# Pairing the 64-token tails of two batches in the channel mix, under a new instruction order

## The chip, the cores and the metric

The kernel runs on one NeuronCore of a Trainium2 chip. The metric is the device time of one execution in microseconds (us). Four runs of the kernel before gave a median of 247.99 us (247.12 to 249.25). The profile is of one further execution.

The engines named below are TensorE (PE in the profile, its weight loads PEld), VectorE (DVE), ScalarE (ACT), GpSimd (POOL) and SyncE (SP). SP does no arithmetic here: it issues every transfer, DMA transposes included, one after the other from one queue.

## The reference

Eight batches of 576 tokens go through an attention of eight heads (a pooled part and a band of seven neighbours) that gives `x`, of 576 tokens by 512 channels. The second half mixes tokens and then channels:

```
theta = x @ w_theta
zr, zi = x * cos(theta), x * sin(theta)
y = einsum('ts,bsd->btd', w_tok_r, zr) + einsum('ts,bsd->btd', w_tok_i, zi)
u = x + y
out = u + maximum(u @ w_ch, 0.0)
```

The change concerns the last line, for tokens 512 to 575 of each batch.

## The kernel before

The work of a batch is cut into small steps. Each kind of step is a generator that walks over all batches in turn, and has one letter. The string `ORDER` says which generator makes its next step; `pin()` then ties every new instruction behind the one before it on the same engine. So `ORDER` fixes the order of the instructions on each engine and of the transfers on SP's queue, and a waiting instruction holds up all that stand behind it on its engine. A step is written here as letter, batch and number: R2.4 is the fifth step of R for batch 2.

| letter | step | engines |
|---|---|---|
| L, v | load of two heads of q or k (8 a batch), of a chunk of v (5) | SP |
| C, w | casts of these to bf16 | POOL (q of batch 0: ACT) |
| A | transposes of q and k, and their pooled sums (4) | PE in batches 0 to 5, ACT, DVE |
| Q, B, N | pooled scores (2), pooled values (1), pooled output (3) | PE, ACT, DVE, POOL |
| S | band scores of a chunk of keys, exponential, two selects that cut the band out (5) | PE, ACT, POOL (not batch 0) |
| V, T | band output of a chunk (5), its transpose and sum into `x` (5) | PE, DVE (POOL for T of 6 and 7) |
| H, Z, z | theta with its sine and cosine (5), products with x (4), turn of the tail's product (1) | PE, ACT, DVE, SP |
| X | token mix: four steps of nine 128x512 matmuls, and one of 36 matmuls for the 64-token tail | PE, DVE |
| u | DMA transposes of u, for the residual (2) | SP |
| R | channel mix of a chunk of tokens (5) | PE |
| O | maximum, residual, store of a chunk (5) | DVE, SP |
| l, c, W, h, g, D, K | weights (loads, casts, turns), warm-up matmuls, constants | all |
| q, t, x | DMA transposes in place of PE ones, batches 6 and 7 | SP |

A batch's 576 tokens are four chunks of 128 and a tail of 64. `mix` (X, L615) adds x to the token mix and leaves `u`, transposed, in `uT`: 512 tokens of four channel blocks, and behind them the four tails. `u_turn` (u, L634) turns both parts back with two DMA transposes (L639, L641). `channels` (R, L646) takes a chunk as the stationary operand: a full chunk needs four 128x512 matmuls (L653). The tail has only 64 columns, so two halves of the output's channels are put at partitions 0 to 63 and 64 to 127 of the same PSUM tile, in eight matmuls of 256 columns (L661). `store` (O, L668) has one DVE instruction a chunk (L675), 512 wide, or 256 wide for the tail, and one store (L681), or two for the tail (L684), each of 64 tokens by two runs of 128 channels.

PSUM and result tiles are few. `w1` hands out four one-bank tiles in rotation (H, T, X, R, Z, W, B and the last step of N), `w2` two two-bank tiles (A, S, Q, V and the first steps of N): a step can't begin on PE before the step that had its tile has been read out. The result tile `osb` of O has four buffers, free again when the store has landed. ScalarE holds one function table: it loads another (`ACT_TABLE_LOAD`) where S or Q follows H, and where H follows S or Q.

Of the kernel before, what the change touches and what calls it, by code (L numbers as in the profile page):

```python
# [10 lines left out]
BF16 = mybir.dt.bfloat16  # L11
AF = mybir.ActivationFunctionType
ALU = mybir.AluOpType
AX = mybir.AxisListType

P = 128
B = 8
H = 8
S = 576
# [22 lines left out]
HALF = 64  # L42
MAIN = 512
# [4 lines left out]
def kernel(  # L48
# [11 lines left out]
    nc = tc.nc  # L60
# [5 lines left out]
    moep = ctx.enter_context(tc.tile_pool(name="moep", bufs=2))  # L66
# [9 lines left out]
    def w1(name, dt=FP32):  # L76
        return ps1.tile([P, 512 if dt == FP32 else 1024], dt, tag="w1" + next(turn1), name=name)


    ORDER = (  # L80
        "LKLLLLLKKCLCCAvCCLvCDwvvvKLCAACwwwwLASCLSVQQCBlLLLLLVSlllllNvlCCCCNlvvvACNVCcScwcvTlTTccllcwAASlHVVH"
        "wwwDTTcAHZHZcHSZcccSDDhLLLzBcCSCWQDVWWLghLLLLCWCCvQvWWLNCNCCWWSWvvLvZNVVXwwwvAAvhwhTXTAALXSwSLLLLXQQ"
        "TBCCVgLggHCuLLVTvHNTVHHZNCCHCCCSwzZZZARRvvvSwOROALSXOLLAAXLLwSwwLvCCCCSCCCCRSNVOXVVXQVTTTAABwSXuTLLA"
        "vvwuvQRvvLLSTSHONNHVLLXuZZANHCLwHwwLVVHRQRRCCCCOzvLLLBOOCCSSTZTCvvRwOTLZSQHVHNVTXTAAXLLACACwCHHwCLCq"
        "LwwqNVHXSZNVXZZvvzSLLCCQCLqXVZLqQvRvwBvOVTVuTTLXTAwASSCHCCHCHNNXqvLwwTwuVXLVLAAHHXqSSZXRQROzONZSCCQC"
        "TCZBSVqROqvvvvZTSSROTVHVRHOTNNTXAAHVHHVwwwwwXAtAXSSzXXSSZZNZVuRuuRRROOQQtOOBRVRVttROtTTTOZOSTNXVRTuN"
        "RRxSSOOOHHVVXtttVHZHZZHNVzZXXttXuXTTXXHTHTTRxROOZHHRuROOHZRZZzOXXXXXXXRuRRRuuOORRuOOROROOORROO"
    )

    staged = {}  # L90
# [86 lines left out]
    for i in range(2):  # L177
        t = const.tile([P, 4, 5, KP], BF16, name=f"kdP{i}")
# [4 lines left out]
    for i in range(2):  # L183
        t = const.tile([P, 4, 5 * 120], BF16, name=f"kT{i}")
# [4 lines left out]
    for i in range(2):  # L189
        t = const.tile([P, NCH, H, 66], BF16, name=f"v_w{i}")  # L190
# [4 lines left out]
    for c in range(NCH):  # L195
        t = const.tile([P, DM], BF16, name=f"tmp{c}")
# [4 lines left out]
    for i in range(2):  # L201
        t = const.tile([P, 2, H, 66], BF16, name=f"vd{i}")
# [12 lines left out]
    wch = wpool.tile([P, 4, DM], BF16, name="wch")  # L215
# [305 lines left out]
    def parted(t):  # L521

        return (t[:, 0:4 * MAIN].rearrange("p (e t) -> p e t", e=4),
                t[:, 4 * MAIN:4 * S].rearrange("p (e t) -> p e t", e=4))
# [85 lines left out]
            yield  # L610


    uTs, urs = {}, {}

    def mix(b):  # L615

        (xA, xB), z = parted(xTs[b]), zs.pop(b)
        uT = uTs[b] = moep.tile([P, 4 * S], BF16, tag="uT", name=f"uT{b}")
        uA, uB = parted(uT)
        for dc in range(4):  # L620
            ps = w1(f"psu{dc}_{b}")
            for j in range(9):
                nc.tensor.matmul(out=ps, lhsT=z[:, j, P * dc:P * dc + P], rhs=WT[:, j, 0:MAIN], start=(j == 0), stop=(j == 8))  # L623
            nc.vector.tensor_tensor(out=uA[:, dc, :], in0=ps, in1=xA[:, dc, :], op=ALU.add)  # L624
            yield
        ps = w1(f"psut_{b}")[:, 0:4 * HALF].rearrange("p (e t) -> p e t", e=4)
        for dc in range(4):
            for j in range(9):
                nc.tensor.matmul(out=ps[:, dc, :], lhsT=z[:, j, P * dc:P * dc + P], rhs=WT[:, j, MAIN:S],  # L629
                                 start=(j == 0), stop=(j == 8))  # L630
        nc.vector.tensor_tensor(out=uB, in0=ps, in1=xB, op=ALU.add)
        yield

    def u_turn(b):  # L634

        ur = moep.tile([P, 16, P], BF16, tag="ur", name=f"ur{b}")
        utr = moep.tile([P, 2, P], BF16, tag="utr", name=f"utr{b}")
        urs[b] = ur, utr
        nc.sync.dma_start_transpose(out=ur, in_=uTs[b][:, 0:4 * MAIN])  # L639
        yield  # L640
        nc.sync.dma_start_transpose(out=utr, in_=uTs[b][:, 4 * MAIN:4 * S])  # L641
        yield

    rels = {}

    def channels(b):  # L646

        uA, uB = parted(uTs[b])
        for c in range(5):
            psr = rels[b, c] = w1(f"psr{c}_{b}")  # L650
            if c < 4:
                for dc in range(4):
                    nc.tensor.matmul(  # L653
                        out=psr, lhsT=uA[:, dc, P * c:P * c + P], rhs=wch[:, dc, :],
                        start=(dc == 0), stop=(dc == 3),
                    )
            else:

                for dc in range(4):
                    for hf in range(2):  # L660
                        nc.tensor.matmul(  # L661
                            out=psr[64 * hf:64 * hf + 64, 0:256], lhsT=uB[:, dc, :],
                            rhs=wch[:, dc, :].rearrange("p (j e d) -> p e j d", j=2, e=2)[:, hf],
                            start=(dc == 0), stop=(dc == 3),
                        )
            yield

    def store(b):  # L668

        ur, utr = urs.pop(b)  # L670
        for c in range(5):
            psr = rels.pop((b, c))
            osb = moep.tile([P, DM], FP32, tag="osb", bufs=4, name=f"osb{c}_{b}")
            n = 4 if c < 4 else 2
            nc.vector.scalar_tensor_tensor(  # L675
                out=osb[:, 0:P * n].rearrange("p (e d) -> p e d", d=P),
                in0=psr[:, 0:P * n].rearrange("p (e d) -> p e d", d=P), scalar=0.0,
                in1=ur[:, c:16:4, :] if c < 4 else utr, op0=ALU.max, op1=ALU.add,
            )
            if c < 4:  # L680
                nc.sync.dma_start(out=out[b, P * c:P * c + P, :], in_=osb)  # L681
            else:
                for hf in range(2):
                    nc.sync.dma_start(  # L684
                        out=out[b, 512:576, :].rearrange("t (j e d) -> e t j d", j=2, e=2)[hf],
                        in_=osb[64 * hf:64 * hf + 64, 0:2 * P].rearrange("p (j d) -> p j d", j=2),
                    )
            yield

    last = {}
# [13 lines left out]
    def batches(steps):  # L709
        for b in range(B):  # L710
            yield from steps(b)

    sequences = dict(L=batches(load), v=batches(load_v), C=batches(cast), w=batches(cast_v), A=batches(turns), B=batches(pooled_v), Q=batches(scores), S=batches(band_scores), N=batches(pooled_out), q=batches(turn_qk), t=batches(turn_x), x=batches(turn_z),
                     V=batches(outputs), T=batches(transposes), H=batches(phases), Z=batches(modulate),
                     K=constants(), z=batches(z_turn), u=batches(u_turn), X=batches(mix), R=batches(channels), O=batches(store),
                     l=weight_loads(), c=weight_casts(), h=channel_loads(), g=channel_casts(), W=weight_turns(), D=warm_up())
    pin()
# [35 lines left out]
```

## Time and profile before

| | |
|---|---|
| median of four runs | 247.99 us |
| the profiled execution: its time | 247.94 us |
| its span, first to last instruction | 246.2 us |
| DVE, ACT, POOL busy | 186.0, 167.0, 161.8 us |
| matmuls of the whole token mix, L623, 288 of them | 66.3 us busy |
| matmuls of the channel mix, full chunks, L653, 128 of them | 31.3 us busy |
| `osb` by DVE, 512 wide, 32 of them | 686 ns each |
| `osb` by DVE, 256 wide, 8 of them | 418 ns each |
| issue of a tail store on SP, L684, 16 of them | 592 ns (median) |
| issue of a full store on SP, L681, 32 of them | 390 ns (median) |
| issue of a tail's transpose on SP, L641, 8 of them | 1193 ns (median) |

The span is 1.7 us shorter than the execution's time. "Busy" is time with at least one instruction of the engine running; a matmul's duration in the groups (379 ns) is longer than the distance from one start to the next (0.216 us for 128x512), because matmuls overlap in the array. The chain of waits gives the distance, and sums are made with it.

### The profile page before, as it was taken

The numbers are of one execution on the slowest core, as the hardware profiler recorded it, in microseconds if no ns is written. First come the engines' busy times: TensorE is split into PE (matmuls) and PEld (weight loads), VectorE is DVE, ScalarE is ACT, GpSimd is POOL, SyncE is SP. The second block draws the span as 40 slices with busy tenths as digits, with TensorE's granted clock in tenths as the row PEclk, the third lists the DMA queues.
The fourth block names the chain that finished last, engine by engine and source line by source line (L and its number), as shares of the span: only waits on it lengthen the run. The fifth ranks groups of instructions, "written<-read, shape, count | busy, mean of one in ns | idle before, by whom it ended". The sixth has DMA issues, their size and how long they took to land. (4 is left out here: it accounts for less than half of the span.)

```text
span 246.2 us, 6608 instructions
## 1 busy us (share of the span) xinstructions
PE 223.4 (91%) x2602; PEld 134.2 (54%) x2602; DVE 186.0 (76%) x345; ACT 167.0 (68%) x248; POOL 161.8 (66%) x223
## 2 busy tenths in 40 slices
PE   0777799999999999999999998999699999999990
PEld 0434554765566567656666555665455655455540
DVE  5275979679879898897989977997687776256462
ACT  3786799757998379998878999899924490350000
POOL 4466477998999999989858764996396943400000
PEclk9999999999999999999999999999989999999999
DMA  6999999999999999999999999199769594946496
GB/s 211 298 270 381 310 212 303 315 232 222 301 214 237 345 229 158 287 255 292 226 186 213 255 227 272 47 201 202 120 156 166 149 209 94 165 166 83 93 260 202
DMA packets 100511, 53.94 MB, mean 219 GB/s; under 512 B 83968, under 2 KB 86016, under 8 KB 100480
## 3 DMA queue, kind: packets, MB, share of 16 engines
q1 hardware_dynamic: 100480, 53.53, 93.8%
q8 instruction: 20, 0.33, 0.6%
q14 instruction: 11, 0.09, 0.2%
HBM read 33.59 MB, written 9.44 MB: 175 GB/s over the span
## 5 line engine op out<-in xcount | busy, mean ns | idle before, releaser
L623 PE MATMUL psu<-WT,z 128*128 128x512 bf16 x288 | 66.3, 379 | 0.5 <-ACT cs L568 0.5
L445 POOL TENSOR_SCALAR_AFFINE_SELECT pm<-pm 128x1024 bf16<-128x1024 bf16 (+1 forms) x35 | 36.8, 1051 | 18.5 <-ACT pm L438 18.5
L438 ACT ACTIVATE pm<-psS 128x1024 bf16<-128x1024 f32 (+1 forms) x40 | 37.7, 980 | 11.6 <-PE psS L430 10.7
L623 PEld LDWEIGHTS <-z 128*128 128x128 bf16 x288 | 26.8, 98 | 29.2 <-issue 0.8
L447 POOL TENSOR_SCALAR_AFFINE_SELECT pm<-pm 128x1024 bf16<-128x1024 bf16 (+1 forms) x35 | 36.7, 1048 | 2.4
L562 PE MATMUL psth<-wth,xT 128*128 128x512 bf16 x128 | 31.5, 379 | 0.1
L624 DVE TENSOR_TENSOR uT<-psu,xT 128x512 bf16<-128x512 f32 x32 | 21.8, 687 | 12.8 <-PE psu L623 12.6
L653 PE MATMUL psr<-wch,uT 128*128 128x512 bf16 x128 | 31.3, 384 | 0.0
L567 ACT ACTIVATE cs<-psth,pihc 128x512 bf16<-128x512 f32 x32 | 22.3, 697 | 11.8 <-PE psth L562 11.3
L131 POOL CAST v_w<-st_v 128x512 bf16<-128x512 f32 (+1 forms) x40 | 24.1, 619 | 9.0 <-DMA st_v<-in_v_dram 9.0
L511 DVE TENSOR_TENSOR tmp<-psloc,rl 120x512 bf16<-120x512 f32 (+2 forms) x40 | 27.6, 691 | 1.4
L342 DVE TENSOR_REDUCE qdT<-qT 128x288 bf16<-128x1152 bf16 x16 | 21.5, 1347 | 8.1 <-ACT qT L334 8.1
L675 DVE SCALAR_TENSOR_TENSOR osb<-psr,ur 128x512 f32<-128x512 f32 x32 | 21.6, 686 | 7.4 <-PE psr L653 6.4
L342 DVE TENSOR_REDUCE kdP<-kT 128x300 bf16<-128x1200 bf16 x16 | 22.4, 1398 | 5.6 <-ACT kT L334 5.6
L124 POOL CAST k_tm<-st_k 128x576 bf16<-128x576 f32 x32 | 21.7, 679 | 5.5 <-DMA st_k<-in_k_dram 5.3
L334 ACT COPY qT<-pstr 128x576 bf16<-128x576 bf16 x24 | 14.2, 646 | 9.2 <-PE pstr L332 9.2
L545 DVE TENSOR_TENSOR xT<-xTps,xdT 128x480 bf16<-128x480 bf16 (+3 forms) x36 | 18.7, 548 | 1.5 <-PE xTps L541 1.1
L124 POOL CAST q_tm<-st_q 128x576 bf16<-128x576 f32 x28 | 18.7, 667 | 1.3 <-PE pstr L332 1.0
L568 ACT ACTIVATE cs<-psth 128x512 bf16<-128x512 f32 x32 | 19.4, 606 | 0.0
L430 PE MATMUL psS<-qT,kT 64*128 64x128 bf16 (+1 forms) x320 | 15.1, 218 | 3.4 <-ACT pm L438 2.2
L653 PEld LDWEIGHTS <-uT 128*128 128x128 bf16 x128 | 11.6, 99 | 12.2 <-issue 0.8
L502 PEld LDWEIGHTS <-pm 128*128 128x128 bf16 (+1 forms) x320 | 14.8, 104 | 4.8 <-issue 0.5
(92 smaller groups left out, 389.9 us busy)
## 6 DMA issues: line engine op xcount, KB each, us to landing
st_q<-in_q_dram SPq DMA_DIRECT2D x32, 288.0 KB, 5.2
st_k<-in_k_dram SPq DMA_DIRECT2D x32, 288.0 KB, 5.3
st_v<-in_v_dram SPq DMA_DIRECT2D x32, 256.0 KB, 5.8
out_dram<-osb SPq DMA_DIRECT2D x32, 256.0 KB, 2.8
st_v<-in_v_dram SPq DMA_DIRECT2D x8, 192.0 KB, 5.1
tok<-in_moe_w_tok_r_dram SPq DMA_DIRECT2D x4, 288.0 KB, 7.7
tok<-in_moe_w_tok_i_dram SPq DMA_DIRECT2D x4, 288.0 KB, 5.8
th<-in_moe_w_theta_dram SPq DMA_DIRECT2D x2, 512.0 KB, 7.2
```

Of the source, the lines that this page charges most:

```text
L124: eng[i](out=dst[:, hh // 2, :, hh % 2, :], in_=staged.pop((b, f"{'qk'[i]}{hh}")).rearrange("p (r d) -> p r d", d=D))
L131: gp(out=v_ws[b % 2][0:KW[c], c, :, 0:D], in_=staged.pop((b, f"v{c}"))[0:KW[c], 0:DM].rearrange("p (h d) -> p h d", d=D))
L342: nc.vector.tensor_reduce(out=dst, in_=src, axis=AX.X, op=ALU.add)
L438: nc.scalar.activation(out=pv, in_=ps[0:kw].rearrange("p e (j w) -> p (e j) w", w=P)[:, :, 0:qn], func=AF.Exp, scale=SCL,)
L445: nc.gpsimd.affine_select(out=pv, in_=pv, compare_op=ALU.is_ge, fill=0.0, base=off, pattern=[[0, 8], [-1, qn]], channel_multiplier=1)
L447: nc.gpsimd.affine_select(out=pv, in_=pv, compare_op=ALU.is_ge, fill=0.0, base=6 - off, pattern=[[0, 8], [1, qn]], channel_multiplier=-1)
L511: nc.vector.tensor_tensor(out=tmp[0:cnt].rearrange("p (e j d) -> p e j d", e=2, j=4), in0=pv[0:cnt, :, :, 0:D], in1=rl[0:cnt].unsqueeze(3) ...
L562: nc.tensor.matmul(out=th, lhsT=xA[:, dc, P * c:P * c + P], rhs=wth[:, dc, :], start=(dc == 0), stop=(dc == 3),)
L567: nc.scalar.activation(out=cs[:, 0, :], in_=th, func=AF.Sin, bias=pihc, scale=1.0)
L623: nc.tensor.matmul(out=ps, lhsT=z[:, j, P * dc:P * dc + P], rhs=WT[:, j, 0:MAIN], start=(j == 0), stop=(j == 8))
L624: nc.vector.tensor_tensor(out=uA[:, dc, :], in0=ps, in1=xA[:, dc, :], op=ALU.add)
L653: nc.tensor.matmul(out=psr, lhsT=uA[:, dc, P * c:P * c + P], rhs=wch[:, dc, :], start=(dc == 0), stop=(dc == 3),)
```

## The change

The tails of an even batch and of the odd one behind it share one chunk.

- `mix` writes the tail into a new tile `uB` that holds both batches' tails, channel block by channel block; `uT` keeps the 512 other tokens.
- `u_turn` turns the tails once for two batches (128x512 in place of twice 128x256), behind the odd batch's main turn. An even batch has one step u, an odd one has two.
- `channels` has four steps R for an even batch and five for an odd one; the fifth takes both tails as 128 columns in four 128x512 matmuls.
- `store` has one 512-wide DVE instruction for both tails, and two stores of 64 rows of 512 channels each.
- `ORDER` has 682 letters in place of 694 (four less of u, R and O), and is new from the first letter to the last. On SP the eighth load of batch 0 goes ahead of its first chunk of v, and both loads of `w_theta` stand behind the first load of batch 1. On PE, S0.2 comes ahead of Q0.0, and A1.0 behind N0.2, V0.2 and T0.0. On ACT, A1.2 comes behind H0.0, and Q1.0 and Q1.1 ahead of S1.1. The number of table loads that H, S and Q ask for stays at 13.

```diff
     ORDER = (
-        "LKLLLLLKKCLCCAvCCLvCDwvvvKLCAACwwwwLASCLSVQQCBlLLLLLVSlllllNvlCCCCNlvvvACNVCcScwcvTlTTccllcwAASlHVVH"
-        "wwwDTTcAHZHZcHSZcccSDDhLLLzBcCSCWQDVWWLghLLLLCWCCvQvWWLNCNCCWWSWvvLvZNVVXwwwvAAvhwhTXTAALXSwSLLLLXQQ"
...
-        "TCZBSVqROqvvvvZTSSROTVHVRHOTNNTXAAHVHHVwwwwwXAtAXSSzXXSSZZNZVuRuuRRROOQQtOOBRVRVttROtTTTOZOSTNXVRTuN"
-        "RRxSSOOOHHVVXtttVHZHZZHNVzZXXttXuXTTXXHTHTTRxROOZHHRuROOHZRZZzOXXXXXXXRuRRRuuOORRuOOROROOORROO"
+        "KKLCLLLKCLCLADLCLCCvvvvCvCKwLAllLLAAwLwSSLwSwLLQBlllllLQcVCCCNCNcVNVTATvvvllvvlAlcCCCCSSHlVVDTccLLcT"
+        "AwLLTZcAHHcLLLLHwZwwZwHcSQDDZQBSWSDcCCcczCCCLvvWVWWWCNCvvNWCWvSWwwWVNVXAAwhvvLTTXALLhAwhXwLLhSSXQQLL"
...
+        "VZqSROTTSSRTVqvvOHHNVTXTNVwwwvAAHHVwwuAXHXASSzXXSSZuRuVRONRQSOOZZZRtttOVQBXVVTTXRttTVRRROTTSSHxOOOHV"
+        "NROtttHVNZZHHXVZzZXNXXXXTTttuTTTRxORHHROOZHZHROHzZZXuXuRXXOXXXRRuRROOOuRROOROOORORO"
     )
...
-    uTs, urs = {}, {}
+    uTs, uBs, urs, utrs = {}, {}, {}, {}
...
-        uT = uTs[b] = moep.tile([P, 4 * S], BF16, tag="uT", name=f"uT{b}")
-        uA, uB = parted(uT)
+        uT = uTs[b] = moep.tile([P, 4 * MAIN], BF16, tag="uT", name=f"uT{b}")
+        uA = uT.rearrange("p (e t) -> p e t", e=4)
+        if b % 2 == 0:
+            uBs[b // 2] = moep.tile([P, 4, 2, HALF], BF16, tag="uB", name=f"uB{b // 2}")
+        uB = uBs[b // 2][:, :, b % 2, :]
...
-        ur = moep.tile([P, 16, P], BF16, tag="ur", name=f"ur{b}")
-        utr = moep.tile([P, 2, P], BF16, tag="utr", name=f"utr{b}")
-        urs[b] = ur, utr
-        nc.sync.dma_start_transpose(out=ur, in_=uTs[b][:, 0:4 * MAIN])
-        yield
-        nc.sync.dma_start_transpose(out=utr, in_=uTs[b][:, 4 * MAIN:4 * S])
-        yield
+        ur = urs[b] = moep.tile([P, 16, P], BF16, tag="ur", name=f"ur{b}")
+        nc.sync.dma_start_transpose(out=ur, in_=uTs[b])
+        yield
+        if b % 2:
+            utr = utrs[b // 2] = moep.tile([P, 4, P], BF16, tag="utr", name=f"utr{b // 2}")
+            nc.sync.dma_start_transpose(out=utr, in_=uBs[b // 2].rearrange("p e i t -> p (e i t)"))
+            yield
...
-        for c in range(5):
+        for c in range(4 + b % 2):
             psr = rels[b, c] = w1(f"psr{c}_{b}")
-            if c < 4:
-                for dc in range(4):
-                    nc.tensor.matmul(
-                        out=psr, lhsT=uA[:, dc, P * c:P * c + P], rhs=wch[:, dc, :],
-                        start=(dc == 0), stop=(dc == 3),
-                    )
-            else:
-
-                for dc in range(4):
-                    for hf in range(2):
-                        nc.tensor.matmul(
-                            out=psr[64 * hf:64 * hf + 64, 0:256], lhsT=uB[:, dc, :],
-                            rhs=wch[:, dc, :].rearrange("p (j e d) -> p e j d", j=2, e=2)[:, hf],
-                            start=(dc == 0), stop=(dc == 3),
-                        )
+            for dc in range(4):
+                nc.tensor.matmul(
+                    out=psr, lhsT=uA[:, dc, P * c:P * c + P] if c < 4 else uBs[b // 2][:, dc],
+                    rhs=wch[:, dc, :], start=(dc == 0), stop=(dc == 3),
+                )
...
-        for c in range(5):
+        for c in range(4 + b % 2):
             psr = rels.pop((b, c))
             osb = moep.tile([P, DM], FP32, tag="osb", bufs=4, name=f"osb{c}_{b}")
-            n = 4 if c < 4 else 2
             nc.vector.scalar_tensor_tensor(
-                out=osb[:, 0:P * n].rearrange("p (e d) -> p e d", d=P),
-                in0=psr[:, 0:P * n].rearrange("p (e d) -> p e d", d=P), scalar=0.0,
-                in1=ur[:, c:16:4, :] if c < 4 else utr, op0=ALU.max, op1=ALU.add,
+                out=osb.rearrange("p (e d) -> p e d", d=P),
+                in0=psr.rearrange("p (e d) -> p e d", d=P), scalar=0.0,
+                in1=ur[:, c:16:4, :] if c < 4 else utrs.pop(b // 2), op0=ALU.max, op1=ALU.add,
             )
             if c < 4:
                 nc.sync.dma_start(out=out[b, P * c:P * c + P, :], in_=osb)
             else:
-                for hf in range(2):
-                    nc.sync.dma_start(
-                        out=out[b, 512:576, :].rearrange("t (j e d) -> e t j d", j=2, e=2)[hf],
-                        in_=osb[64 * hf:64 * hf + 64, 0:2 * P].rearrange("p (j d) -> p j d", j=2),
-                    )
+                for i in range(2):
+                    nc.sync.dma_start(out=out[b - 1 + i, 512:576, :], in_=osb[HALF * i:HALF * i + HALF])
```

More of the change, by code (lines that the diff above doesn't have):

```diff
@@ L80 @@
     ORDER = (
-        "LKLLLLLKKCLCCAvCCLvCDwvvvKLCAACwwwwLASCLSVQQCBlLLLLLVSlllllNvlCCCCNlvvvACNVCcScwcvTlTTccllcwAASlHVVH"
-        "wwwDTTcAHZHZcHSZcccSDDhLLLzBcCSCWQDVWWLghLLLLCWCCvQvWWLNCNCCWWSWvvLvZNVVXwwwvAAvhwhTXTAALXSwSLLLLXQQ"
-        "TBCCVgLggHCuLLVTvHNTVHHZNCCHCCCSwzZZZARRvvvSwOROALSXOLLAAXLLwSwwLvCCCCSCCCCRSNVOXVVXQVTTTAABwSXuTLLA"
-        "vvwuvQRvvLLSTSHONNHVLLXuZZANHCLwHwwLVVHRQRRCCCCOzvLLLBOOCCSSTZTCvvRwOTLZSQHVHNVTXTAAXLLACACwCHHwCLCq"
-        "LwwqNVHXSZNVXZZvvzSLLCCQCLqXVZLqQvRvwBvOVTVuTTLXTAwASSCHCCHCHNNXqvLwwTwuVXLVLAAHHXqSSZXRQROzONZSCCQC"
-        "TCZBSVqROqvvvvZTSSROTVHVRHOTNNTXAAHVHHVwwwwwXAtAXSSzXXSSZZNZVuRuuRRROOQQtOOBRVRVttROtTTTOZOSTNXVRTuN"
-        "RRxSSOOOHHVVXtttVHZHZZHNVzZXXttXuXTTXXHTHTTRxROOZHHRuROOHZRZZzOXXXXXXXRuRRRuuOORRuOOROROOORROO"
+        "KKLCLLLKCLCLADLCLCCvvvvCvCKwLAllLLAAwLwSSLwSwLLQBlllllLQcVCCCNCNcVNVTATvvvllvvlAlcCCCCSSHlVVDTccLLcT"
+        "AwLLTZcAHHcLLLLHwZwwZwHcSQDDZQBSWSDcCCcczCCCLvvWVWWWCNCvvNWCWvSWwwWVNVXAAwhvvLTTXALLhAwhXwLLhSSXQQLL"
+        "TBVHVTHNHTNCHuggCLgVCZCwwHCgZAZCLCCSXZzRLvLvvAvvLLLLLSROOANCACLLXSCCwwwCSRCwCSCORVVOXVLAXATBSSXQVTTT"
+        "AQTSHVvwvvHuNXvvNZAHNLLVVHTHRCwwwCCLQQCRRzOuOOZSBLLLLLSCCTvSCvCZTRSHOVNHZVZNXTTAvvAXAwAHVHCCCwwwwCLL"
+        "CqHSXLLqCNVZXZVCLSBXZzLqTCTQQLLLqTRuVVAAvvvvXOSSHXCCCNNTLXwCwCVLTVAAwwwqHHHHSSvvXzXZZZQLRBSCCQRqCOON"
+        "VZqSROTTSSRTVqvvOHHNVTXTNVwwwvAAHHVwwuAXHXASSzXXSSZuRuVRONRQSOOZZZRtttOVQBXVVTTXRttTVRRROTTSSHxOOOHV"
+        "NROtttHVNZZHHXVZzZXNXXXXTTttuTTTRxORHHROOZHZHROHzZZXuXuRXXOXXXRRuRROOOuRROROOORORO"
     )
@@ L644 @@
     rels = {}
     def channels(b):
-        uA, uB = parted(uTs[b])
-        for c in range(5):
+        uA = uTs[b].rearrange("p (e t) -> p e t", e=4)
+        for c in range(4 + b % 2):
             psr = rels[b, c] = w1(f"psr{c}_{b}")
-            if c < 4:
-                for dc in range(4):
-                    nc.tensor.matmul(
-                        out=psr, lhsT=uA[:, dc, P * c:P * c + P], rhs=wch[:, dc, :],
-                        start=(dc == 0), stop=(dc == 3),
-                    )
-            else:
-                for dc in range(4):
-                    for hf in range(2):
-                        nc.tensor.matmul(
-                            out=psr[64 * hf:64 * hf + 64, 0:256], lhsT=uB[:, dc, :],
-                            rhs=wch[:, dc, :].rearrange("p (j e d) -> p e j d", j=2, e=2)[:, hf],
-                            start=(dc == 0), stop=(dc == 3),
-                        )
+            for dc in range(4):
[3 more added lines that the diff above has]
+                )
@@ L666, in channels @@
             yield
     def store(b):
-        ur, utr = urs.pop(b)
-        for c in range(5):
+        ur = urs.pop(b)
+        for c in range(4 + b % 2):
             psr = rels.pop((b, c))
             osb = moep.tile([P, DM], FP32, tag="osb", bufs=4, name=f"osb{c}_{b}")
-            n = 4 if c < 4 else 2
             nc.vector.scalar_tensor_tensor(
-                out=osb[:, 0:P * n].rearrange("p (e d) -> p e d", d=P),
-                in0=psr[:, 0:P * n].rearrange("p (e d) -> p e d", d=P), scalar=0.0,
-                in1=ur[:, c:16:4, :] if c < 4 else utr, op0=ALU.max, op1=ALU.add,
+                out=osb.rearrange("p (e d) -> p e d", d=P),
+                in0=psr.rearrange("p (e d) -> p e d", d=P), scalar=0.0,
+                in1=ur[:, c:16:4, :] if c < 4 else utrs.pop(b // 2), op0=ALU.max, op1=ALU.add,
```

## The prediction

> **What bounds the kernel now.** I read the head of the page first, then the busy time by stretches, the chain of waits, and the timelines of single engines.
>
> ```profile
> span 246.2 us, 6608 instructions
> PE 223.4 (91%) x2602; PEld 134.2 (54%) x2602; DVE 186.0 (76%) x345; ACT 167.0 (68%) x248; POOL 161.8 (66%) x223
> ```
>
> PE is busy for 91% of the span, but that is a mean over stages. The windows, with cuts at 50 (where X0.0 starts), 131.4, 177 and 232.5 us (the end of X7.4), show the limits:
>
> ```profile
> 0.00:50.00 50.00, 37.34 (x471) 23.27 (x472) 34.29 (x85) 37.08 (x58) 32.38 (x56) 1.00 1.02 287
> 50.00:131.40 81.40, 80.43 (x1060) 51.44 (x1059) 71.88 (x122) 66.07 (x106) 74.11 (x101) 1.00 1.05 245
> 131.40:177.00 45.60, 42.20 (x505) 25.16 (x503) 38.51 (x66) 44.28 (x56) 30.91 (x41) 1.00 1.01 194
> 177.00:232.50 55.50, 55.30 (x525) 30.72 (x525) 34.64 (x64) 19.58 (x33) 24.46 (x28) 0.97 0.71 142
> 232.50:246.20 13.70, 8.12 (x48) 3.57 (x46) 6.72 (x11) 0.00 (x0) 0.00 (x0) 0.98 0.76 216
> ```
>
> The columns after the length are busy us of PE, PEld, DVE, ACT and POOL, then the granted clock. PE rules from 50 to 131.4 (80.4 of 81.4) and from 177 to 232.5 (55.3 of 55.5). From 131.4 to 177 it is ACT, with 44.3 of 45.6; PE idles 3.4 us there. The opening belongs to no engine: PE idles 12.7 us. The last 13.7 us are stores. That the third stretch ends on ACT is seen on PE's timeline, where S7.0 waits for the exponential of S6.3:
>
> ```profile
> 176.53 0.40 PE L430 MATMUL psS<-qT,kT 64*128 64x128 bf16 x8 [1.91 <-ACT pm L438]
> ```
>
> The chain of waits has start, duration and work, and gives what a tail costs beside full chunks:
>
> ```profile
> 180.01 3.89 PE psr L653 x16
> ...
> 184.89 0.56 PE psr L661 x8
> 185.44 0.36 PE psloc L502 x8
> 185.81 0.86 PE psr L653 x4
> ...
> 239.62 2.25 DMA out_dram<-osb
> ...
> 241.98 0.42 DVE osb L675
> ```
>
> Four full matmuls take 0.86 us of the chain, the eight half-wide ones of a tail 0.56. Near the end DVE waits for a store to land before it has a result tile.
>
> **The change, part by part.** Where an end is one of idle time, the trace of before can't say what a new order makes of it, so I give both ends.
>
> *Tail matmuls.* Eight groups of 0.56 us go (4.5 us), four of 0.86 come (3.4 us): 1.0 us of PE's work less. But it counts only where PE rules. Even batches lose 0.56 each, odd ones gain 0.30. [...] The measured 0.56 is 1.5 times better than 0.86, not twice, and so some saving is left.
>
> *DVE.* Eight of 418 ns (3.3 us) become four of 686 ns (2.7 us). Hidden: DVE has 9.5 us free from 50 to 131.4 and 20.9 us from 177 to 232.5. Without that cover it would be a gain of 0.6.
>
> *SP.* Sixteen tail stores of 0.59 us and eight tail turns of 1.19 us go (19.0 us of issue); eight stores like L681's (0.39) and four turns as wide as the 128x512 turn of z, L590 (1.23) come (8.0 us). Before the tail SP mostly waits for POOL's casts, so the 11 us hide there.
>
> *Waits added.* The shared turn and R of the odd batch need both X tails. R1.4 stands 121 letters behind X1.4, so nothing is held. X4.4 writes the `uB` that R1.4 and u1.1 read; both stand well before. On SP, u7.1 stands behind O6.2, and O6.3 and all of O7 queue behind it, as before.
>
> *The new order in the opening, to X0.0.* The eighth load goes ahead of v, so A0.3 no longer waits 1.42 us for `k_tm`; but its PSUM tile is A0.1's, read until 12.01, and ACT's copies are strung together anyway. ACT gains the 0.37 us it idled there. S0.0 to S0.2, Q0.0, B0.0 and Q0.1 then follow on ACT (1.94, 1.02, 0.89, 0.88, 0.64, from 14.6) to 20.0. N0.0 takes Q0.1's PSUM tile, so it starts then (19.85 before). N0.0 and N0.1 need 2 us of PE, DVE's two divisions end at 23.1, and then N0.2, V0.2 and T0.0 (0.26 to 0.5 each) stand ahead of A1.0: it starts at 24.3, not 22.14. This is the row to compare with:
>
> ```profile
> 22.84 1.18 ACT L334 COPY qT<-pstr 128x576 bf16<-128x576 bf16 x2 [2.01 <-PE pstr L332]
> ...
> 27.23 1.18 ACT L334 COPY kT<-pstr 128x576 bf16<-128x576 bf16 x2 [1.17 <-PE pstr L332]
> ...
> 30.20 1.28 ACT L567 ACT_TABLE_LOAD   x1
> ```
>
> Behind A1.0 the work is denser: A1.1, S0.3 and S0.4 (1.1, 1.0, 0.8) follow it on ACT without the idle 0.47 and 1.17 us of before, and the table load starts at 28.9, 1.3 us early. But A1.2 (1.2) is then still to come, and ACT waits some 0.4 us for it, since D.1 (1.3) stands before it on PE. S1.0's exponential starts 0.3 us late (39.6). Q1.0 and Q1.1 ahead of S1.1 cost PE 0.1 us, because D.2 and D.3 (2.76 us of warm-up) cover them. I take **+0.4 us**. The lower end is -1.4, the whole wait for `k_tm`. The upper is +2.9: the 1.64 us of idle are not won back, and S1.1 waits behind Q1.0's exponential (0.9).
>
> *From 50 to 131.4.* R0.4 goes: **-0.56**. The order could at best remove PE's idle 0.97 us, or add as much: -1.5 to +0.4.
>
> *From 131.4 to 177.* R2.4 goes and R1.4 grows, but ACT has the same work, and PE's saving becomes more waiting at S7.0. Only ACT's idle 1.3 us can shrink: 0.67 for S6.1's scores and 0.56 before H5.0, with R2.4 and R2.2 on PE nearby. New is that A6.2 and A6.3 (2.33 and 2.32 us) stand ahead of H4.1 on ACT, so H4.1's to H4.4's PSUM tiles are read out later and X3.3 waits some 0.8 us on PE, in a stretch where PE has time. I take **-0.3**; ends -1.3 (no idle left) and +2.2 (one more stall as long as that at 176.53, 1.91, and the 0.27 behind it).
>
> *From 177 to 232.5.* R4.4 goes (-0.56), R3.4 and R5.4 grow (+0.60): **+0.04**. X5.0 and X5.1 come earlier, and X5.0 needs Z5.3, which DVE ends just in time; up to +0.5. The clock belongs here too:
>
> ```profile
> 174.00:180.00 6.00, 3.82 (x67) 3.42 (x64) 4.61 (x7) 5.59 (x7) 3.31 (x4) 0.78 0.73 147
> 180.00:186.00 6.00, 6.00 (x59) 2.78 (x57) 4.03 (x8) 1.76 (x3) 4.81 (x5) 0.94 0.49 143
> ```
>
> A granted clock of 0.78 and 0.94 over 6 us each cost up to 1.3 + 0.4 = 1.7 us of PE's pace, right behind the stall of 2.2 us; I leave this dip as it is, with 0 and 1.7 as what it can give back. [...]
>
> *The tail.* From X7.3's result at 232.17 both orders run alike to O6.1's store (issued 234.98). Result tiles are reused every fourth time. O6.2's store is issued at 235.84 (before: 236.81, behind u7.1), then u7.1 to 237.4, then O6.3's store; with some 2.5 us to land behind the turn's data it lands at 240.3, and O7.3 takes its tile. O7.0 takes O6.0's (landed 237.72), and its store, no longer behind two tail stores (1.23 us), is issued at 238.5 and lands at 240.9 (241.86 before). O7.4 follows O7.3 on DVE at 241.2, now 686 ns and not 418; its two stores issue from 242.0 to 242.75 (before 242.44 to 243.63) and land at 244.8 instead of 245.1: **-0.3**. Ends: -1.0 (O6.3 lands as early as 239.35, its neighbour of before) and +0.5 (the wider turn holds the stores behind it).
>
> **The sum**, on the profiled execution's 247.94 us (span 246.2, and 1.7 around it; the median of the runs, 247.99, is the same within 0.05): 247.94 + 0.4 - 0.56 - 0.3 + 0.04 - 0.3 = **247.2 us**.
>
> **Rivals.** *Slower, by the opening.* One mechanism: the four steps N0.2, V0.2, T0.0 and A1.2 moved around A1.0 and H0.0 starve ACT between 20 and 40 us, and everything behind X0.0 starts later. For it: ACT already idles 2.01 us before A1.0, and I move A1.0 by 2.1. Against it: it idled 1.64 us later on, which I let vanish. At its price of +2.9 the sum is 249.7. It turns the sign once the opening costs over 1.1 us. *Faster, by the third stretch.* If the new order has PE's scores ready a little earlier, so that ACT never idles, and the stall at 176.53 shrinks until the clock holds, -1.0 more there and up to -1.7 of clock: half of the latter gives 245.4. [...] Against it: ACT's work in that stretch is the same, and A6.2 and A6.3 were moved forward. *The change saves, but nothing arrives:* the 1.0 us of matmuls only lengthens PE's waits and the wider last turn and store eat the tail's gain: 248.0 to 248.3. This is inside the likeliest case's own range.
>
> **How the numbers follow.** The sum as worked out has 0.44 (own range 246.2 to 248.5), the slower rival 0.34, the faster 0.22. A measurement of this kernel can't tell less than about 0.5%, that is 1.24 us, from no change: 246.75 to 249.23. Of the 0.44, some 0.14 lies below, 0.29 within, 0.01 above; of the slower rival 0.03 lies within. So faster 0.36, no change 0.32, slower 0.32. The range has to reach both rivals: 244.8 to 250.6, the upper end being the opening's +2.9 with a part of the third stretch's +2.2.
>
> **What would show it.** In the trace after: X0.0 at 50.2 (opening), and ACT's first table load for H near 28.9; four groups `psr` of 128 columns more and no L661; ACT busy over 44 us in the 45 us before S7.0, with a wait of PE there of at least 1.9 us; PE without gaps from S7.1 to R7.4; and, from R7.4's end to the span's end, less than the 5.6 us of before. The prediction is wrong if X0.0 moves by over 1.5 us, or if the stall before S7.0 goes or comes twice.

## The result and the profile after

The changed kernel takes 249.15 us (median of 44 runs, 247.31 to 250.55), the kernel before 247.89 beside it (63 runs, 246.02 to 249.71). The ratio is 1.0052, with a 95% interval of 1.0038 to 1.0066: half a per cent slower. The forecast was 247.2, with a range of 244.8 to 250.6. A ratio here is worked out from the single runs without those that lie over 1.5% above the fastest of their kernel (three of twelve in the kernel with both fills, one of 29 beside it), so it isn't the quotient of two medians.

The profiled execution took 249.63 us. First the head of its page, then the busy time by stretches, with cuts where X0.0 starts, A6.0 starts on ACT, S7.0 starts on PE, and X7.4 ends. The columns are those of the windows shown before.

```profile
span 247.9 us, 6488 instructions
...
PE 225.0 (91%) x2554; PEld 135.7 (55%) x2554; DVE 185.8 (75%) x341; ACT 166.5 (67%) x248; POOL 161.6 (65%) x223
```

```profile
0.00:51.40 51.40, 39.58 (x470) 25.90 (x471) 33.87 (x86) 36.55 (x57) 31.60 (x55) 0.93 1.01 275
51.40:133.20 81.80, 80.60 (x1048) 51.44 (x1045) 73.63 (x120) 66.08 (x106) 74.84 (x103) 1.00 1.01 246
133.20:178.75 45.55, 41.53 (x494) 24.71 (x493) 37.52 (x65) 43.87 (x56) 30.24 (x39) 1.00 0.90 185
178.75:234.60 55.85, 55.58 (x517) 30.35 (x517) 34.18 (x63) 20.00 (x33) 24.95 (x28) 0.97 0.65 147
234.60:247.90 13.30, 7.73 (x36) 3.33 (x34) 6.63 (x10) 0.00 (x0) 0.00 (x0) 0.98 0.86 229
```

PE has 1.0 us of matmuls less to do, and yet is busy 1.6 us longer (225.0 against 223.4). The first row tells why: its granted clock is 0.93, where the opening of before had 1.00. The same five points in both profiles (us; the first line is PE's first matmul, the others are distances from one point to the next):

| | before | after | difference | forecast |
|---|---|---|---|---|
| PE's first matmul | 6.63 | 7.27 | +0.64 | 0 |
| to X0.0 | 43.19 | 44.14 | +0.95 | +0.4 |
| to A6.0 on ACT | 81.56 | 81.79 | +0.23 | -0.56 |
| to S7.0 on PE | 45.15 | 45.55 | +0.40 | -0.3 |
| to the end of X7.4 | 55.96 | 55.81 | -0.15 | +0.04 |
| to the end of the span | 13.74 | 13.32 | -0.42 | -0.3 |

The first line is no part of the change. The start of the first matmul lay between 5.92 and 7.31 us in the twelve profiles that follow, in either order: 5.92 to 7.25 with the old opening, 5.95 to 7.31 with the new. So profiles are compared from the first matmul on; from there the forecast's terms add up to -0.72 us, and the differences measured to +1.01.

PE's timeline in the opening of after (start, duration, work, in brackets the idle time before it and what ended it):

```profile
18.76 0.24 PE L382 MATMUL psSd<-qdT,kdP 64*128 64x144 bf16 x2 [0.37 <-ACT pm L438]
...
19.54 0.41 PE L502 MATMUL psloc<-v_w,pm 128*128 128x65 bf16 x8 [0.31 <-ACT pd L392]
20.75 0.43 PE L464 MATMUL psnd<-vd,pd 128*72 128x65 bf16 x8 [0.79 <-ACT pd L409]
...
22.82 0.62 PE L502 MATMUL psloc<-v_w,pm 128*128 128x65 bf16 x8 [0.52 <-DVE xd L477]
...
24.91 1.17 PE L332 MATMUL pstr<-ident,q_tm 128*128 128x128 bf16 x9
```

No wait is as long as 0.8 us. But they stand close together, and from 22.2 us on, ahead of the last one shown, PE runs at half its clock: the nine transposes of A1.0 take 1.17 us, where the groups of before took 0.66 and 0.67. Two windows of after, cut at the point where the clock falls, and one of before behind its stall at S7.0:

```profile
18.80:22.20 3.40, 2.07 (x38) 1.49 (x37) 1.22 (x4) 1.90 (x4) 1.91 (x3) 1.00 1.06 394
22.20:29.10 6.90, 6.23 (x62) 4.81 (x62) 5.43 (x10) 3.16 (x6) 6.20 (x10) 0.51 1.09 336
```

```profile
177.30:180.80 3.50, 3.50 (x39) 2.75 (x37) 2.44 (x5) 2.32 (x3) 3.36 (x5) 0.51 0.81 150
```

With the windows set exactly on the dips, the one in the opening lasts 6.83 us (22.21 to 29.04), and the one that both kernels have behind S7.0 lasts 3.41, both at 0.50. In between PE's clock is 1.00. On ACT this gives (after):

```profile
24.30 0.64 ACT L490 COPY xdT<-psxd 128x576 bf16<-128x576 bf16 x1 [3.61 <-PE psxd L487]
26.11 1.18 ACT L334 COPY qT<-pstr 128x576 bf16<-128x576 bf16 x2 [1.17 <-PE pstr L332]
...
30.69 1.28 ACT L567 ACT_TABLE_LOAD   x1
```

ACT waits 3.61 us for PE's turn of N0's result, and 1.17 us more for A1.0's slow transposes. Counted from the first matmul, the table load comes at 23.42 us, 0.15 earlier than before (23.57) and not 1.3.

### The profile page after: what moved, and what is told of

Same layout as the page of the kernel before. It is cut to its first block, busy times and chain, and to the rows that moved or that the text cites. A ratio compares the mean times of both kernels' runs of the same rounds, so it can differ in the third digit from the quotient of the medians.

```text
span 247.9 us, 6488 instructions
## 1 busy us (share of the span) xinstructions
PE 225.0 (91%) x2554; PEld 135.7 (55%) x2554; DVE 185.8 (75%) x341; ACT 166.5 (67%) x248; POOL 161.6 (65%) x223
## 4 chain that ended last, share of the span: by engine, by line
PE 68%; ACT 10%; DMA 8%; SPq 6%; POOL 3%; issue 1%; DVE 1%; DVEq 0%; POOLq 0%; ACTq 0%
PE psu L626 21%; PE psr L655 10%; PE psth L562 10%; PE psloc L502 4%; PE psS L430 4%; SPq L110 4%; PE pstr L332 3%; DMA st_k<-in_k_dram 3%; PE psut L632 2%; DMA ur<-uT 2%; ACT kT L334 2%; DMA out_dram<-osb 2%; SPq L101 2%; ACT qT L334 2%; PE xTps L541 2%; DMA tok<-in_moe_w_tok_i_dram 2%
## 5 line engine op out<-in xcount | busy, mean ns | idle before, releaser
L655 PE MATMUL psr<-wch,uT 128*128 128x512 bf16 x128 | 32.1, 388 | 0.0
L502 PEld LDWEIGHTS <-pm 128*128 128x128 bf16 (+1 forms) x320 | 15.5, 106 | 6.5 <-issue 1.3
L605 DVE TENSOR_TENSOR z<-psxt,cs 128x1024 bf16<-128x1024 bf16 x24 | 16.0, 682 | 3.2 <-PE psxt L604 3.1
```

The costliest lines, as they stand in the source:

```text
L502: nc.tensor.matmul(out=pv[0:qn, h // 4, h % 4, :], lhsT=pms[b][c][0:kw, 4 * par + blk, 0:qn], rhs=v_w[0:kw, c, h, 0:65], start=(h % 4 == 0 ...
L655: nc.tensor.matmul(out=psr, lhsT=uA[:, dc, P * c:P * c + P] if c < 4 else uBs[b // 2][:, dc], rhs=wch[:, dc, :], start=(dc == 0), stop=(dc ...
```

## The experiments

Two questions were open: which part of the change costs the time (the pairing, the opening, or the new order behind it), and whether the opening costs it by its order or by the clock.

**The pairing alone.** The paired tails in the old order, with u, R and O of the even tails left out of it.

```diff
-... SXOLLAAXLL ... TTTAABwSXuTLLAvvwuvQRvvLLSTSHONNH ...
+... SXOLLAAXLL ... TTTAABwSXTLLAvvwuvQvvLLSTSHNNH ...
```

> The pairing alone, under the old order: the twelve letters that it drops are struck out, the other 682 stay where they were. Theory 1 (the opening of the new order costs the time, the pairing saves): 0.3 to 0.9 us faster than before, ratio 0.9965 to 0.9990, X0.0 at 49.8 us as before. Theory 2 (the pairing itself costs: a wider last turn, chunk and store): 1.2 us slower, ratio about 1.005. Theory 3 (the new order costs a little everywhere): as theory 1.

Measured: 247.28 us (12 runs) beside 247.48; ratio 1.0002 (0.9971 to 1.0034). By itself the pairing is worth nothing that can be measured, though the interval reaches some 0.8 us either way. Where it went is seen at R0.4's place. PE's timeline of this kernel has S3.3 behind the gap:

```profile
93.52 0.40 PE L430 MATMUL psS<-qT,kT 64*128 64x128 bf16 x8 [0.86 <-ACT qT L334]
```

and that of before:

```profile
93.55 0.40 PE L430 MATMUL psS<-qT,kT 64*128 64x128 bf16 x8 [0.31 <-ACT qT L334]
```

The step starts at the same time, and the wait for ACT's copy of `qT` has grown by 0.55 us, which is R0.4's 0.56. PE is busy for 98.8% of that stretch, yet this one step stood in the 1%. The pair's wider R1.4 comes dear on the other hand, as it stands ahead of B5.0, for which ACT waits; this kernel and then before, on ACT:

```profile
131.12 0.59 ACT L355 CAST vd<-psva 128x512 bf16<-128x512 f32 x1 [0.72 <-PE psvb L353]
```

```profile
130.74 0.59 ACT L355 CAST vd<-psva 128x512 bf16<-128x512 f32 x1 [0.31 <-PE psvb L353]
```

ACT's next step, A6.0, comes 0.38 us later, and the third stretch is ACT's. R2.4 becomes waiting as well: S6.4, at 171.73, waits 0.73 us for DVE, and S7.0 1.70, where before S7.0 alone waited 1.91.

**The old opening, and the new one alone.** The first is the changed kernel with the old order up to X0.0, the second the kernel of before with the new order up to X0.0 (unpaired). The few loads and casts that the two openings don't share stand behind X0.0 in both.

```diff
 first, against the changed kernel
-"KKLCLLLKCLCLADLCLCCvvvvCvCKwLAllLLAAwLwSSLwSwLLQBlllllLQcVCCCNCNcVNVTATvvvllvvlAlcCCCCSSHlVVDTccLLcT"
+"LKLLLLLKKCLCCAvCCLvCDwvvvKLCAACwwwwLASCLSVQQCBlLLLLLVSlllllNvlCCCCNlvvvACNVCcScwcvTlTTccllcwAASlHVVH"
...
 second, against the kernel of before
-"LKLLLLLKKCLCCAvCCLvCDwvvvKLCAACwwwwLASCLSVQQCBlLLLLLVSlllllNvlCCCCNlvvvACNVCcScwcvTlTTccllcwAASlHVVH"
+"KKLCLLLKCLCLADLCLCCvvvvCvCKwLAllLLAAwLwSSLwSwLLQBlllllLQcVCCCNCNcVNVTATvvvllvvlAlcCCCCSSHlVVDTccLLcT"
...
```

> The changed kernel with the old order up to X0.0, and the new one from there. Theory 1: the loss is gone, 0 to 0.6 us faster than before, ratio 0.9975 to 1.000, X0.0 at 49.8 us, granted clock 1.00 from 18 to 30 us. Theory 2: still 1.2 us slower, ratio 1.005. Theory 3: 0.5 to 0.9 us slower, ratio 1.002 to 1.0035.

> The kernel before with the new order up to X0.0 alone. Theory 1: 1.2 to 1.8 us slower than before, ratio 1.005 to 1.0075, X0.0 near 51.4 us, granted clock under 0.8 between 21 and 30 us. Theory 2: no change. Theory 3: 0.4 to 0.9 us slower, ratio 1.0015 to 1.0035.

Measured: the old opening 248.42 us, ratio 1.0046 (1.0017 to 1.0076); the new opening alone 248.37, ratio 1.0036 (1.0006 to 1.0066), 12 runs each beside 247.48. So the new opening is slower by itself, but taking it out doesn't bring the changed kernel back, and the two losses add up to 0.8%. Their intervals reach down to the changed kernel's 0.5%, so the third theory, a little everywhere, isn't excluded; the first, that the opening is all, is. The second has the dip of the clock too, though it falls at another time:

```profile
16.30:19.70 3.40, 1.89 (x35) 1.14 (x31) 0.90 (x2) 2.63 (x5) 1.64 (x4) 1.00 1.02 384
19.70:26.70 7.00, 6.60 (x65) 5.05 (x64) 5.01 (x10) 2.63 (x5) 5.07 (x8) 0.51 1.06 370
```

The second has X0.0 43.62 us behind its first matmul, 0.43 later than before. The first has no dip there (a granted clock of 1.00 from 18 to 30 us), and X0.0 at 43.22, as before.

**The new order with the tails unpaired.** The steps of the even tails are put back, each behind the last step that it needs.

```diff
-... XSCCwwwCSRCwCSCORVVOXVLAXATBSSXQVTTT ...
+... XSCCwwwCSRCwCSCORRVVOOXVLAXATBSSXQVTTT ...
```

> The new order with the old tails: the twelve letters are put back, each behind the step that it needs. Theory 1: 1.3 to 2.0 us slower than before, ratio 1.005 to 1.008, with X0.0 at 51.4 us. Theory 2: no change, ratio 0.999 to 1.001. Theory 3: 1.3 to 2.0 us slower, but the distance from X0.0 to the end longer than in the kernel before by 0.5 us or more.

Measured: 260.34 us (6 runs), ratio 1.0539 (1.0496 to 1.0582). This tells nothing of the pairing. DVE's timeline shows what the tail does where it was put:

```profile
92.98 0.42 DVE L675 SCALAR_TENSOR_TENSOR osb<-psr,utr 128x256 f32<-128x256 f32 x1 [8.21 <-DMA out_dram<-osb]
```

O0.4 waits 8.2 us for the store that holds its result tile, and that store stands on SP's queue behind loads; meanwhile PE gets no work for 7.7 us. A step of 0.42 us, in a wrong place, waits twenty times its length.

**The opening kept warm.** The changed kernel with nine matmuls of 128x512 on constants, in the four places where PE waits between 17 and 23 us (one ahead of Q0.1, one of V0.0, four of N0.0, three of V0.1). The unchanged changed kernel ran beside it.

```diff
+    def short_warm():
+
+        for i in range(4):
+            ps = w1(f"wd{i}")
+            for _ in range([1, 1, 4, 3][i]):
+                nc.tensor.matmul(out=ps, lhsT=ident, rhs=warm, start=True, stop=True)
+            yield
...
-... LLQBlllllLQcVCCCNCNcVNV ...
+... LLQBlllllLdQcdVCCCdNCNcdVNV ...
```

> The changed kernel with nine more warm-up matmuls in the waits that PE has between 18 and 23 us (one before Q0.1, one before V0.0, four before N0.0, three before V0.1). Theory 1a (the opening loses by PE's clock, which falls because PE waits too often there): granted clock 1.00 from 18 to 30 us, X0.0 0.5 to 0.7 us sooner after the first matmul than in the changed kernel (43.5 us, not 44.1), 0.4 to 0.8 us faster than the changed kernel. Theory 1b (it loses by ACT waiting for A1.0, whatever the clock): clock 1.00 too, but X0.0 still 44.0 us or more after the first matmul, and no faster.

> The changed kernel as it is, beside the others, for a second profile of it: every theory expects 1.003 to 1.007 of before; theory 1a expects the clock under 0.8 between 21 and 27 us again.

Measured: 247.37 us, ratio 0.9987 (0.9957 to 1.0016); the changed kernel beside it 248.48, ratio 1.0041 (1.0014 to 1.0067); before 247.98. More work for PE made the changed kernel 1.1 us faster (248.48 - 247.37). None of the twelve runs has a mean granted clock under 0.982, where ten of the twelve beside it have 0.981 or less. The window that had 2.07 us of work now has 3.24, and the clock holds:

```profile
18.80:22.20 3.40, 3.24 (x36) 1.91 (x34) 1.84 (x5) 1.28 (x4) 2.52 (x4) 1.00 1.05 390
```

ACT, with the two times that the prediction named:

```profile
24.67 1.18 ACT L342 COPY qT<-pstr 128x576 bf16<-128x576 bf16 x2 [0.55 <-PE pstr L340]
...
28.73 1.28 ACT L575 ACT_TABLE_LOAD   x1
```

The transposes of A1.0 start at 23.97, the table load stands at 28.73, and X0.0 42.70 us behind the first matmul (after: 44.14; before: 43.19). At full clock the new opening is 0.5 us shorter than the old one. ACT's long wait for N0's result is still 3.40 us, so it belongs to the order and not to the clock; what goes is the wait for A1.0's transposes, from 1.17 to 0.55.

The second profile of the changed kernel agrees with the first to 0.1 us up to 22.8 us, but its dip comes later and is half as long:

```profile
19.70:23.10 3.40, 1.87 (x36) 1.35 (x35) 2.05 (x6) 1.04 (x3) 2.77 (x5) 1.00 1.07 397
23.10:26.70 3.60, 3.23 (x44) 3.10 (x41) 2.83 (x6) 1.19 (x3) 3.10 (x6) 0.53 1.06 383
```

Its X0.0 stands 43.65 us behind the first matmul, not 44.14. All fourteen profiles, from the last transposes of batch 0 (A0.3) to X0.0, so that the start of the kernel is left out:

| opening | dip there | profiles | A0.3 to X0.0, us |
|---|---|---|---|
| old | none | 7 | 37.05 to 37.29 |
| new, with the nine matmuls | none | 3 | 36.91 in each |
| new | 3.41 us | 1 | 37.73 |
| new | 6.83 us | 3 | 38.13 to 38.21 |

So the dip costs the new opening 0.8 us when it is short and 1.2 to 1.3 when it is long. A0.3 itself starts 5.36 to 5.93 us behind the first matmul in the new opening and 5.85 to 6.14 in the old; that spread is why X0.0 came 0.95 us late in one profile with the long dip, and 0.30 and 0.43 in the two others.

**The stall at S7.0 filled.** Eight such matmuls ahead of S7.0, in the paired kernel of the old order and in the kernel of before.

```diff
-... AXSSzXXSSZZNZV ...
+... AXSSzXXdSSZZNZV ...
```

> The pairing under the old order, with eight warm-up matmuls (1.7 us) in PE's wait before S7.0, so that the clock has no reason to fall behind it. If the dip of the clock at 177 to 186 us is worth what it seems (1.3 + 0.4 us): granted clock 1.00 to the end, S7.0 to the end of X7.4 in 54.3 us and not 56.0, 0.8 to 1.7 us faster than before (ratio 0.993 to 0.997). If what follows S7.0 doesn't hang on PE's clock: no change from the pairing under the old order (0.999 to 1.001).

> The kernel before, with the same eight warm-up matmuls before S7.0. As with the pairing: 0.8 to 1.7 us faster than before if the dip costs what it seems, no change if not. Whatever it gains, the pairing with the same fill (the run beside it) should differ from it by less than 0.5 us if the pairing is worth nothing, and gain 0.5 to 1.0 more if its saved matmul time reaches the end once the stall is out of the way.

Measured: 247.19 us, ratio 0.9992 (0.9966 to 1.0018), and 246.98, ratio 0.9969 (0.9938 to 0.9999), beside 247.98. In both profiles the dip behind S7.0 is gone (a granted clock of 1.00 from 177 to 200 us). The two against each other again show nothing for the pairing.

**Clock and time, run by run.** Each run's record has its mean granted clock. It falls in steps of some 0.007, which is what one dip of 3.41 us at half the clock takes from 247 us (3.41 * 0.5 / 247). Not every step is a dip in the work: in the profiles the clock also falls in the last microseconds, while PE has little left or nothing to do (at 245.63 us of 246.2 in that of before, at 247.49 of 247.9 in that of after; the paired kernel in the old order has 0.994 by a fall at 242.1 us alone). The runs of before beside the experiments, and those of the changed kernel, by clock (runs, median us):

```
mean clock        before         changed
0.996 and more    18  246.50      -
0.989 to 0.995    31  247.20      3  247.51
0.982 to 0.988    34  248.22      1  248.20
0.973 to 0.981     9  248.74     48  249.00
under 0.973        -              4  249.93
all               92  247.55     56  249.01
```

From row to row the time grows by 0.5 to 1.0 us. The kernel before has none, one or two of them in 83 of 92 runs; the changed kernel has three or more in 52 of 56. In one row of the table the two differ by some 0.3 us or less, though the changed kernel has only 3 runs and 1 in two of the three shared rows: the difference of the medians goes with that of the clock. The table alone doesn't show which makes which; the nine matmuls do, for the opening.

**Which parts are worth having, with the clock held.** Four kernels, all with eight matmuls ahead of S7.0: the kernel of before with the new opening (with its nine matmuls); the changed kernel with both fills; and the paired kernel with the new order from A6.0 only, and from X0.0 only.

```diff
 first, against the kernel of before
-"LKLLLLLKKCLCCAvCCLvCDwvvvKLCAACwwwwLASCLSVQQCBlLLLLLVSlllllNvlCCCCNlvvvACNVCcScwcvTlTTccllcwAASlHVVH"
+"KKLCLLLKCLCLADLCLCCvvvvCvCKwLAllLLAAwLwSSLwSwLLQBlllllLdQcdVCCCdNCNcdVNVTATvvvllvvlAlcCCCCSSHlVVDTcc"
...
-... AXSSzXXSSZZNZV ...
+... AXSSzXXdSSZZNZV ...
 second, against the changed kernel
-... LLQBlllllLQcVCCCNCNcVNV ...
+... LLQBlllllLdQcdVCCCdNCNcdVNV ...
-... XASSzXXSSZuRuV ...
+... XASSzXXdSSZuRuV ...
 third and fourth, against the changed kernel: the old order up to A6.0, and up to X0.0, and
-... XASSzXXSSZuRuV ...
+... XASSzXXdSSZuRuV ...
```

> The kernel of before with the new order up to X0.0, kept warm by nine short warm-up matmuls in PE's waits, the old order from there on, tails unpaired, and eight warm-up matmuls ahead of S7.0. Nothing of the output changes. The first theory (the new opening is by itself 0.5 us shorter, and loses more than that because the granted clock falls there): X0.0 starts 42.7 us after the first matmul (before: 43.2), mean clock 0.993, and the time is the filled old kernel's 246.98 less 0.5: ratio 0.995. The rival (the new opening is no shorter, the warm-up matmuls only repay what they cost): ratio 0.997, as for the old kernel with only the eight.

> The changed kernel with the nine warm-up matmuls in the opening and the eight ahead of S7.0. Nothing of the output changes. First theory (the clock is the whole loss; at full clock the changed kernel and the old one are equal): mean clock 0.993, 246.3 to 246.6 us, ratio 0.994 to 0.995. Rival (the new order behind X0.0 costs 0.6 us at any clock): 247.0, ratio 0.997, and 0.002 above the kernel with the old order behind X0.0 beside it.

> Paired tails, the old order up to A6.0 and the new one from there on, eight warm-up matmuls ahead of S7.0. Nothing of the output changes. If the new order's cost behind X0.0 lies in the stretch of ACT (A6.2 and A6.3 ahead of H4.1): A6.0 to S7.0 45.5 us, ratio 1.001, like the kernel with the new order from X0.0. If it lies before A6.0: 45.15 us, ratio 0.999, like the paired kernel in the old order with the same eight matmuls.

> Paired tails, the old order up to X0.0 and the new one from there on, eight warm-up matmuls ahead of S7.0. Nothing of the output changes. If the new order behind X0.0 costs time at any clock: ratio 1.001 to 1.002, about 0.6 us above the paired kernel in the old order with the same eight matmuls (0.999). If what it lost was the clock alone: 0.997 to 0.999.

Measured, beside 247.91 for the kernel before:

| kernel | us (runs) | ratio, 95% interval |
|---|---|---|
| new opening, old rest, unpaired | 246.05 (6) | 0.9926, 0.9897 to 0.9956 |
| changed kernel, both fills | 248.04 (12) | 0.9954, 0.9914 to 0.9994 |
| paired, new from A6.0 | 246.99 (12) | 0.9979, 0.9956 to 1.0002 |
| paired, new from X0.0 | 246.72 (12) | 0.9971, 0.9944 to 0.9998 |

The first beats both kernels: its six runs lay from 244.75 to 246.31. Part of that is the fill ahead of S7.0, which alone gave 0.9969. Its windows have the clock at 1.00 at both places:

```profile
18.00:24.00 6.00, 5.38 (x76) 3.42 (x76) 3.52 (x10) 2.60 (x6) 4.31 (x7) 1.00 1.06 393
...
174.00:180.00 6.00, 5.55 (x85) 3.60 (x82) 4.80 (x8) 5.64 (x7) 3.15 (x4) 1.00 0.79 144
```

The second fell into two groups of runs, five from 245.0 to 245.9 us and seven from 248.0 to 249.8, all at a mean clock of 0.993 to 1.000; the profile is one of the first group. What the others lost isn't seen, and the mean clock doesn't tell them apart. Its median and its ratio therefore say little; the five are no slower than the six runs of the first kernel. The third and fourth don't differ. In the third the stretch from A6.0 to S7.0 is 45.56 us long, in the fourth 45.54, in the paired old order 45.16: the 0.4 us that the new order costs there belong to the steps from A6.0 on. But the times don't show it as a loss: the fourth, all new behind X0.0, is at 0.9971 no slower than the old order with the same fill (0.9992). In the profiles the 0.4 us is made up behind S7.0, where the stretch to the end of X7.4 is 54.34 us long in both and 54.85 in the old order. The cost of the changed kernel with the old opening (1.0046) was thus not found again once the stall at S7.0 was filled. Its runs had a mean clock of 0.9885, hardly less than the 0.9895 of before beside it, so the clock explains little of the 1.0046, which is 0.8 to 0.9 us (0.4 to 1.9 by the interval). Its profile shows 0.38 us from A6.0 to S7.0 (45.53 against 45.15); what else there is stays open.

## Why the prediction was wrong

The prediction was wrong in its sign: slightly faster forecast, 0.5% slower measured. In the profile, counted from the first matmul, it was off by 0.55 us in the opening, by 0.79 and 0.70 in the two stretches behind it, and by -0.19 and -0.12 in the last two. The other 0.64 us of the profile's loss is the later first matmul, which is chance.

**The step that failed is the opening, "I take +0.4 us".** Its working priced each group of PE at the duration that it had before, at a clock of 1.00. The clock was weighed behind S7.0 and put at nothing here, though the same order that delays A1.0 brings five waits of 0.2 to 0.8 us within 5 us. What the runs showed in its place is a dip that costs 0.8 to 1.3 us. The forecast had 4.6 us from A1.0's start to the table load; measured were 5.78, and 4.76 once the waits were filled and the clock held. The terms for ACT's order were on the other side too high: with the clock held X0.0 comes 0.5 us early (42.70), where they gave 0.4 late. The two errors have opposite signs, so it is luck that three of the four profiles of this opening, with 0.30, 0.43 and 0.46, lie near the +0.4. A1.0's start was luck too: 24.3 forecast, and 24.91 - 0.64 = 24.27 measured, counted from the first matmul, but with the clock down for 2.7 us by then; with the clock held it is 0.46 us earlier.

Over the runs the changed kernel has one to two steps of the clock more than before, at some 0.7 us each, which is about the 1.2 us of the whole loss. That sum is no proof for the whole: the kernel with the old opening lost 0.8 to 0.9 us at nearly the mean clock of before. Shown is that the changed kernel loses about 1.1 us by the dip in its opening, as the nine matmuls take that much away.

**"From 50 to 131.4: -0.56" failed.** It was +0.23. A stretch in which PE is busy for 98.8% isn't a stretch in which every step of PE counts: R0.4 stood just ahead of a wait for ACT, and filled it. The paired kernel in the old order showed this by itself. The term was also too large as a sum: R1.4, which grows by 0.30, was counted behind 131.4, but it stood at 129.66 before and ahead of A6.0 in the new order too, so that PE saved 0.26 us here and not 0.56.

**"From 131.4 to 177: -0.3" failed, but its reading held.** PE's saving became waiting, as forecast: S7.0 waits

```profile
178.75 0.40 PE L430 MATMUL psS<-qT,kT 64*128 64x128 bf16 x8 [1.96 <-ACT pm L438]
```

But ACT's idle time, which I let shrink by 0.3, grew from 1.32 to 1.68 us: 0.77 and 0.56 us at the two places that had 0.67 and 0.56, and two new waits of 0.15 and 0.12. That is nearly all of the stretch's 0.40 us, and five other kernels with the new order there repeat it (45.53 to 45.56 us). X3.3's forecast wait of 0.8 us was 0.29.

**"From 177 to 232.5: +0.04" was right** within 0.2 (-0.15). Leaving the dip as it is was right for this profile. The price of 1.7 for its whole gain was right too: the paired old order's profile has no dip (1.00 from 176.9 to 231.3 us), and its stretch is 54.37 us long, 1.6 less. Over the runs the fill was worth less, 1.0 us at the medians in the kernel of before (246.98 against 247.98) and 0.1 in the paired one (247.19 against 247.28, on two different chips). That not every run has the dip may be the reason.

**The tail, -0.3, was right** at -0.42. The last links of the chain of after:

```profile
234.56 2.60 PE psr L655 x12
237.36 2.33 DMA out_dram<-osb
...
240.25 2.30 DMA out_dram<-osb
242.67 0.70 DVE osb L667
243.40 0.69 DVE osb L667
```

O7.4 was forecast at 241.2 with X7.4's end at 232.49, that is 8.7 us behind it; it came 8.84 behind it, 686 ns wide as costed, and still behind a store for O7.3's tile.

**The rivals.** The slower one named the right place and sequence (A1.0 late, ACT starved between 20 and 30 us: 3.61 and 1.17 us of idle), but not the cause, as the 3.40 and 0.55 of the clock held go with an opening that is shorter than the old one; and its price of 2.9 was the end of the range, where the loss was 0.95. The faster one, through the third stretch, didn't come: the stall before S7.0 neither shrank nor lost its dip. "Saves but nothing arrives" describes the matmuls truly: the pairing alone is 1.0002.

**A sign of being wrong.** The prediction named X0.0 moving by over 1.5 us. X0.0 came at 51.41, 1.59 us later, but only 0.95 of that lies behind the first matmul.

**What isn't settled.** Why the long dip costs 1.2 to 1.3 us in the opening, though 6.83 us at half speed would be 3.4 us of full matmul pace, was not tried by itself; that part of it falls in time in which PE would have waited anyway is an argument only. The nine matmuls also take four of the rotating PSUM tiles, which is a full turn of the four; that they help by anything but the clock was not tried apart. The two groups of runs of the doubly filled kernel and the loss of the one with the old opening are open as well.

## What to carry to other kernels

In a new order, look for the density of short waits on TensorE, not only for their sum on the critical path: where waits under 0.8 us each left TensorE 1.87 to 2.07 us of work in 3.4, the clock of the new opening went to half for 3.41 or 6.83 us, and nine matmuls on constants in their place took 1.1 us off the kernel. A saving on an engine that is busy for 99% of a stretch was worth nothing where the removed step stands ahead of a wait; look at what its successor would then wait for. And a reordering that looks slower can hide a gain: with the clock held there and at S7.0, the same opening gave 0.9926 of the time before, against 0.9969 with S7.0 alone.

## What the runs showed of the chip

The granted clock has two values in these traces, 1.00 and 0.50, and within the work it holds the lower one for 3.41 us or for 6.83 (the windows above, set in tenths, show 0.51 and 0.53). In the profile of after the clock falls at 22.21, 179.22 and 247.49 us, the second 157.01 us behind the first and the third 68.27 behind the second, 46 and 20 times the 3.413 us of a short dip; in that of before it falls at 177.36 and 245.63, also 68.27 apart. What sets the moment of a fall was not shown. Ahead of the three dips in the opening whose windows stand above PE had been busy for 2.07, 1.89 and 1.87 us of the last 3.4; the longest single wait there was 0.79 (after, and the new opening alone). Nine of the 92 runs of before in the table have a mean clock of 0.979, and no profile shows where these lost it. The old opening comes near the new one (1.86 us of work in its thinnest 3.4 us) and had no dip in any of its profiles:

```profile
25.40:28.80 3.40, 1.86 (x27) 1.42 (x24) 2.88 (x7) 2.23 (x4) 2.26 (x3) 1.00 1.15 339
```

So no sharp bound on the busy share can be read from this: 1.86 us of work went without a dip, 1.87 and 1.89 with one. The mean clock of one order differs from run to run (0.979 to 0.999 for before), and where the dip falls moves (19.8 and 20.7 us in two profiles of the new opening, 22.2 and 23.2 in the two others).
